# A new order for the same 1738 steps of a decaying linear attention with a feed-forward block behind it

## The chip, the cores and the metric

The kernel runs on one core of a Trainium2 chip. What counts is the time of one execution on the device, in microseconds (us). Three executions of the kernel before took 564.64, 563.89 and 563.01 us; the median is 563.89 us.

A core has a matrix engine (TensorE, PE in the profile), a vector engine (VectorE, DVE), an engine for activation functions (ScalarE, ACT), a general one (GpSimd, POOL) and one that here only issues transfers (SyncE, SP). Each works through its own queue of instructions in order and waits where an instruction needs something that another engine or a transfer has not delivered yet.

## The reference

Attention with a complex, per-position decay is a recurrence over 768 positions, for 4 sequences and 8 heads of 48 dimensions. What comes out is turned into 3072 tokens of 384 features and goes through a feed-forward block with 2048 hidden features.

```
a_n = a * min(|a|, 0.999) / (|a| + 1e-6)          # complex a = a_re + i a_im
for t in range(S):
    S_re, S_im = a_n[t] * (S_re + i S_im) + k[t] v[t]^T
    y[t] = einsum('bhd,bhde->bhe', q[t], S_re)
x = y.transpose(0, 2, 1, 3).reshape(B * S, H * D)
h = x @ w_in
out = (h * (1 / (1 + exp(-1.702 * h)))) @ w_out
```

## The kernel before

**Units.** The 3072 tokens are cut into 12 units of 256 tokens, three to a sequence, each of two chunks of 128 (c = 0 and 1). For every unit the kernel turns the recurrence into matmuls: `prepare` scales and rotates queries and keys by running products and running angles of the decay (scans, L356, L376 and L396 on VectorE; logarithms and sines on ScalarE). Ten transfers (`remap`, L447 to L450), here called the moves, then bring queries and keys of all heads into place in `qkh`. `attend` (L455 on) does the rest for each chunk: 32 small matmuls per half of the heads give the scores (L511, into `p_ps` and `z_ps`), VectorE masks them (`pm`, L517), eight transposes turn the keys (L530), ScalarE copies them (`kt`, L534), small matmuls mix the masked scores and the state with the values into `x_ps` (L501), and others build the new state in `z_ps` (L553, taken over at L569 or L573; the decay of the state is L472). `x_ps` is copied out at L559 and, for the lower half of the precision, at L563. TensorE splits an fp32 matmul into two records in the trace.

**Feed-forward block.** `moe` works on groups of units: unit 0 alone, unit 1 alone, then pairs. Its hidden blocks (L650, into `h_ps0` and `h_ps1`) and its projections (L681, into `o_ps0` to `o_ps2`) are the large matmuls: 128 columns in group 0, 256 in group 1, 512 in the five others. "H1.3" is the hidden block numbered 3 of the group that begins with unit 1. Group 0 uses whole fp32 weights. From group 1 on each weight is split into a high part (L267, ScalarE) and a low part (L272, VectorE), each value of the hidden layer likewise into `gh` (L663) and `gl` (L667), and three products are summed. The silu is at L659 for group 0 and at L663 and L665 for the others.

**Weights.** Sixteen raw blocks of weights, called f0 to f15, are loaded at L245 into four raw buffers in turn and converted there by VectorE (L247, L250, L254) and ScalarE (L253). f11 takes the buffer that f7 had, f13 that of f9.

**What sets the order.** Every piece of work is handed to a plan as a step with its engine, what it reads and what it writes; there are 1738. A table, `ORDER`, lists their numbers. `Plan.order` reads the table and makes sure that no step stands ahead of one that it needs; the loop at the end emits the steps in that order. Each engine's queue is therefore the table, reduced to the steps of that engine; a step of SyncE issues one load or all five transfers of one half of the moves. Where the table of ScalarE's functions has to change between two steps, a load of it (L881) is put in. Thirteen warm-up matmuls (L432) with no use for the result stand ahead of TensorE's work.

```
for n in order:
    o = plan.ops[n]
    if o[5] not in (None, cur):
        nc.scalar.preload_act_table_set(o[5])
        cur = o[5]
    o[3]()
```

## Time and profile before

| | |
|---|---|
| three executions | 564.64, 563.89, 563.01 us; median 563.89 |
| span of the profiled execution | 563.3 us |
| TensorE busy | 527.2 us, 94% |
| VectorE busy | 389.4 us, 69% |
| ScalarE busy | 370.5 us, 66% |
| first matmul starts | 23.10 us |
| last large matmul ends | 558.6 us |
| loads of ScalarE's function tables | 58, 74.4 us in all |

The profile is of one execution. Its page gives busy times and shares for each engine; a matmul's end is modelled, so the duration of a group of matmuls is best read from the starts of what comes before and after. A row of a timeline gives a start, a duration, engine and line, what was written from what, how many, and in brackets how long the engine had stood idle just before and for whom. [...]

### The profile page before, as it was taken

The page shows a single profiled execution, that of the slowest core. Times are in us where ns is not written, and L with a number is a line of the kernel's source. Part 1 is how long each engine was busy: PE and PEld are TensorE (multiplying, and loading weights), DVE is VectorE, ACT ScalarE, POOL GpSimd, SP SyncE. Part 2 cuts the span into 40 slices and gives each one's busy share as a digit, 9 for nine tenths or more (in the row PEclk, how much of TensorE's full clock was granted, in tenths as well). Part 3 has the DMA queues.
Part 4 walks back from the last instruction along what each step waited for, and adds up shares of the span by engine and source line. Part 5 has one row for each costly group of instructions (what it writes and reads, how often), then busy time and mean ns, then how long its engine had stood idle before and what let it go on. Part 6 is the DMA issues. An engine that isn't in the chain of part 4 may idle for free.

```text
span 563.3 us, 14541 instructions
## 1 busy us (share of the span) xinstructions
PE 527.2 (94%) x6204; PEld 447.8 (79%) x6204; DVE 389.4 (69%) x625; ACT 370.5 (66%) x561; POOL 12.0 (2%) x55
## 2 busy tenths in 40 slices
PE   0379799999999999999999999999999999999996
PEld 0368799999988887888888888888888888888885
DVE  7999899999989886977857756654685442243223
ACT  7888789999798979687769667355944221323321
POOL 6000000000000000000000000000000000000000
PEclk9999989999999999999999999999999999999999
DMA  8579993727275756576257355336417013231001
GB/s 333 170 210 358 189 363 68 238 58 197 91 183 189 178 168 171 198 171 201 77 129 243 105 131 162 115 78 154 151 61 185 29 45 101 65 96 45 29 28 61
DMA packets 29270, 82.04 MB, mean 146 GB/s; under 512 B 4112, under 2 KB 7184, under 8 KB 29200
## 3 DMA queue, kind: packets, MB, share of 16 engines
q1 hardware_dynamic: 29200, 81.06, 49.5%
q8 instruction: 50, 0.82, 0.6%
q14 instruction: 20, 0.16, 0.1%
HBM read 57.41 MB, written 4.72 MB: 110 GB/s over the span
## 4 chain that ended last, share of the span: by engine, by line
PE 60%; ACT 1%; DVE 1%; issue 0%; ACTq 0%
PE o_ps L681 26%; PE h_ps L650 25%; PE x_ps L501 4%; PE z_ps L511 1%; PE p_ps L511 1%; PE z_ps L553 1%; PE p_ps L530 1%; PE z_ps L530 1%; DVE qr L229 0%; DVE qk L229 0%; DVE gl L667 0%; ACT L881 0%; ACT h_ps L665 0%; ACT s L333 0%; ACT s L331 0%
## 5 line engine op out<-in xcount | busy, mean ns | idle before, releaser
L667 DVE TENSOR_TENSOR gl<-h_ps,gh 128x512 fp32r<-128x512 f32 x88 | 60.1, 687 | 116.4 <-ACT h_ps L665 113.0
L663 ACT ACTIVATE gh<-h_ps 128x512 fp32r<-128x512 f32 x88 | 52.4, 596 | 133.9 <-PE h_ps L650 105.7
L650 PE MATMUL h_ps<-xhi,hiA 128*128 128x512 f32 (+1 forms) x288 | 109.0, 379 | 0.5 <-DVE gl L667 0.5
L650 PE MATMUL h_ps<-xlo,hiA 128*128 128x512 f32 (+1 forms) x288 | 107.2, 372 | 0.0
L650 PE MATMUL h_ps<-xhi,loA 128*128 128x512 f32 (+1 forms) x288 | 107.1, 372 | 0.0
L681 PE MATMUL o_ps<-gh,hiU 128*128 128x512 f32 (+1 forms) x288 | 80.5, 380 | 0.0
L681 PE MATMUL o_ps<-gl,hiU 128*128 128x512 f32 (+1 forms) x288 | 80.2, 379 | 0.0
L681 PE MATMUL o_ps<-gh,loU 128*128 128x512 f32 (+1 forms) x288 | 78.2, 372 | 0.0
L881 ACT ACT_TABLE_LOAD x58 | 74.4, 1283 | 1.9 <-PEq L1126 0.9
L650 PEld LDWEIGHTS h_ps<-xhi,hiA 128*128 128x128 f32 x288 | 54.2, 188 | 11.1 <-DVE gl L667 1.1
L650 PEld LDWEIGHTS h_ps<-xhi,loA 128*128 128x128 f32 x288 | 54.2, 188 | 9.6
L650 PEld LDWEIGHTS h_ps<-xlo,hiA 128*128 128x128 f32 x288 | 54.3, 188 | 9.2 <-DVE xlo L563 0.3
L681 PEld LDWEIGHTS o_ps<-gh,loU 128*128 128x128 f32 x288 | 52.2, 188 | 9.8
L681 PEld LDWEIGHTS o_ps<-gh,hiU 128*128 128x128 f32 x288 | 51.0, 188 | 11.0 <-issue 2.0
L681 PEld LDWEIGHTS o_ps<-gl,hiU 128*128 128x128 f32 x288 | 50.9, 188 | 9.7 <-issue 0.8
L665 ACT ACTIVATE h_ps<-h_ps 128x512 f32<-128x512 f32 x88 | 51.8, 591 | 0.1
L229 DVE TENSOR_TENSOR qk<-qk,s 128x768 f32<-128x768 f32 (+2 forms) x39 | 43.9, 1133 | 3.2 <-ACT s L425 2.2
L501 PE MATMUL x_ps<-pm,v 128*32 128x128 f32 x768 | 38.9, 276 | 1.4 <-DVE pm L517 1.4
L715 DVE TENSOR_REDUCE fit<-raw_w 128x1 f32<-128x384 f32 x64 | 33.6, 543 | 5.2 <-DMA raw_w<-in_w_out_dram 5.2
L501 PE MATMUL x_ps<-qkh,st 96*32 96x128 f32 x640 | 33.0, 272 | 0.0
L681 PE MATMUL o_ps<-g,valU 128*128 128x128 f32 x192 | 26.3, 289 | 4.3 <-ACT g L659 3.2
L432 PE MATMUL h_ps<-qk,ident 128*128 128x256 f32 x26 | 8.0, 456 | 23.1 <-DVE s L415 23.1
(104 smaller groups left out, 778.6 us busy)
## 6 DMA issues: line engine op xcount, KB each, us to landing
v<-in_v_dram SPq DMA_DIRECT2D x24, 416.0 KB, 4.0
ri<-in_a_dram SPq DMA_DIRECT2D x11, 768.0 KB, 5.9
qk<-in_qk_dram SPq DMA_DIRECT2D x11, 768.0 KB, 6.8
qkh<-qr SPq DMA_DIRECT2D x22, 288.6 KB, 5.9
qkh<-qk SPq DMA_DIRECT2D x22, 288.6 KB, 5.5
raw<-in_w_in_dram SPq DMA_DIRECT2D x8, 768.0 KB, 6.5
raw<-in_w_out_dram SPq DMA_DIRECT2D x8, 768.0 KB, 5.6
raw_w<-in_w_in_dram SPq DMA_DIRECT2D x16, 384.0 KB, 3.5
```

Source lines behind the costliest of these rows:

```text
L229: add(en, t, rank, lambda: e.tensor_tensor(out=out, in0=a, in1=b, op=alu), **kw)
L432: add("PE", 0.43, -WARM + k, lambda k=k, dst=dst: mm(h_ps[0][:, k % 2 * T : (k % 2 + 1) * T], lhsT=ident, rhs=dst[:, k % NR, 0:T], start=T ...
L501: mm(x_ps[32 * j : 32 * j + 32, r, :], lhsT=lt, rhs=rt, start=n == 0, stop=n == len(steps) - 1)
L511: mm(ps_[to : to + QL, j, lo:L], lhsT=at(h, 1, c)[:, lo : lo + QL], rhs=at(h, 0, c)[:, lo:L], start=True, stop=True)
L530: nc.tensor.transpose(banks[h // 4][0][:, h % 4, 0:KD], at(h, 1, c), ident[0:KD, 0:KD])
L650: mm(h_ps[hb][:, k * n_x : (k + 1) * n_x], lhsT=ww[:, r * T + f * P : r * T + (f + 1) * P], rhs=x[:, r, xs], start=n == 0, stop=n == last)
L663: add("ACT", a_t(CW) - 0.13, rk(order_), lambda hb=hb, gb=gb: act(out=high.g(gb), in_=h_ps[hb], func=AF.Silu, scale=SLOPE), r=[f"h{hb}"], ...
L665: add("ACT", a_t(CW) - 0.13, rk(order_), lambda hb=hb: act(out=h_ps[hb], in_=h_ps[hb], func=AF.Silu, scale=SLOPE), w=[f"h{hb}"], tab=SILU, ...
L667: add("DVE", d_t(CW), rk(order_), lambda hb=hb, gb=gb: dve.tensor_tensor(out=glo[gb], in0=h_ps[hb], in1=high.g(gb).bitcast(F32), op=ALU.su ...
L681: mm(o_ps[c][:, xs], lhsT=y[:, f * DM + c * P : f * DM + (c + 1) * P], rhs=x[:, k * n_x : (k + 1) * n_x], start=i == 0 and f == 0 and n == ...
L715: add("DVE", d_t(CK), rk + 2, lambda x=x, op=op: dve.tensor_reduce(out=f_w[:, x, n : n + 1], in_=weights.looked_at()[:, :, 1], op=op, axis ...
L881: nc.scalar.preload_act_table_set(o[5])
```

## The change

The table `ORDER` is replaced by another permutation of the same step numbers that keeps every dependency. Nothing else is touched: the same steps, tiles, buffers and, but for waits and one more table load (59 instead of 58), the same instructions. Two lines of the table, of 73:

```diff
 ORDER = """
-80 5 128 0 100 10 82 81 84 83 85 86 6 87 7 8 94 129 88 9 130 92 89 25
...
+80 5 128 10 100 0 82 81 84 83 85 86 8 6 7 87 88 9 89 90 92 25 94 130
...
```

Three places in which the queues differ follow. In all rows the number behind a name is that of the buffer or tile.

SyncE's queue ahead of the moves of unit 1 (the last five rows of each piece are their first half; `raw_72` to `raw_75` are the four raw buffers; the second `raw_75` from `in_w_in_dram` is f11, `raw_72` and `raw_74` from `in_w_out_dram` are f8 and f10). Before:

```order
L245 DMA raw_75<-in_w_in_dram 128x1536
L324 DMA ri<-in_a_dram 128x1536
L245 DMA raw_72<-in_w_out_dram 128x1536
L607 DMA v_86<-in_v_dram 128x832
L245 DMA raw_74<-in_w_out_dram 128x1536
L245 DMA raw_75<-in_w_in_dram 128x1536
L447 DMA qkh_76<-qr 48x1539 x2
L448 DMA qkh_76<-qr 32x2x513
L450 DMA qkh_76<-qr 16x513 x2
```

and in the new order:

```order
L382 DMA qk<-in_qk_dram 128x3x512
L324 DMA ri<-in_a_dram 128x1536
L245 DMA raw_73<-in_w_in_dram 128x1536
L245 DMA raw_75<-in_w_in_dram 128x1536
L245 DMA raw_72<-in_w_out_dram 128x1536
L245 DMA raw_74<-in_w_out_dram 128x1536
L447 DMA qkh_76<-qr 48x1539 x2
L448 DMA qkh_76<-qr 32x2x513
L450 DMA qkh_76<-qr 16x513 x2
```

f11 has moved from the last place ahead of the moves to a place ahead of f8 and f10, behind f9 (`raw_73`); the load of the values of unit 1 (`v_86`) has gone behind the moves.

VectorE's queue at the hidden block H1.3, which overwrites `h_ps_108` and reads the low half of the weight block A3 (`loA_1319` before, `loA_1122` now). Before:

```order
L472 TENSOR_TENSOR st_93<-st_93,qkh_77 96x4x2x48
L272 TENSOR_TENSOR loU_1280<-valU_482,hiU_568 128x768
L667 TENSOR_TENSOR gl_100<-h_ps_108,gh_1224 128x512
L229 TENSOR_TENSOR qk<-qk,s_83 128x3x256
L415 TENSOR_SCALAR s_82<-s_85 128x3
L272 TENSOR_TENSOR loA_1319<-valA_257,hiA_695 128x768
L229 TENSOR_TENSOR qk<-qk,s_81 128x3x256
```

and in the new order:

```order
L272 TENSOR_TENSOR loA_1122<-valA_233,hiA_534 128x768
L699 TENSOR_SCALAR osb_101<-o_ps_109 128x256
L409 SCALAR_TENSOR_TENSOR s_85<-s_85,s_82 128x3x256
L699 TENSOR_SCALAR osb_103<-o_ps_111 128x256
L699 TENSOR_SCALAR osb_102<-o_ps_110 128x256
L667 TENSOR_TENSOR gl_99<-h_ps_107,gh_1129 128x512
L356 SCALAR_TENSOR_TENSOR s_81<-s_84,s_83 128x257 x3
L364 TENSOR_SCALAR small<-s_81 128x3
L365 RECIPROCAL small<-small 128x3
L376 SCALAR_TENSOR_TENSOR s_83<-s_84,small,s_83 128x256 x3
L517 TENSOR_TENSOR pm_95<-p_ps,mask 128x512
L667 TENSOR_TENSOR gl_100<-h_ps_108,gh_1168 128x512
```

The low half of A3 has moved from the third row behind `gl_100` to the first row here, eleven ahead of it.

TensorE's queue at unit 6, chunk 1 (`qkh_77`): its scores for the second half of the heads (`z_ps`). Before, with 27 large matmuls since the last small one:

```order
L681 MATMUL o_ps_110<-gh_1224,loU_1818 128x512
L681 MATMUL o_ps_110<-gl_100,hiU_1121 128x512
L511 MATMUL z_ps<-qkh_77 32x128 x4
L511 MATMUL z_ps<-qkh_77 32x96 x4
L511 MATMUL z_ps<-qkh_77 32x64 x4
L511 MATMUL z_ps<-qkh_77 32x32 x4
L650 MATMUL h_ps_107<-xhi_926,hiA_756 128x512
L650 MATMUL h_ps_107<-xlo_92,hiA_756 128x512
L650 MATMUL h_ps_107<-xhi_926,loA_1085 128x512
```

and in the new order:

```order
L511 MATMUL p_ps<-qkh_77 32x128 x4
L511 MATMUL p_ps<-qkh_77 32x96 x4
L511 MATMUL p_ps<-qkh_77 32x64 x4
L511 MATMUL p_ps<-qkh_77 32x32 x4
L501 MATMUL x_ps<-pm_96,v_86 32x128 x4
L511 MATMUL z_ps<-qkh_77 32x128 x4
L511 MATMUL z_ps<-qkh_77 32x96 x4
L511 MATMUL z_ps<-qkh_77 32x64 x4
L511 MATMUL z_ps<-qkh_77 32x32 x4
L681 MATMUL o_ps_109<-gh_1129,hiU_1109 128x512
L681 MATMUL o_ps_110<-gh_1129,hiU_1109 128x512
L681 MATMUL o_ps_111<-gh_1129,hiU_1109 128x512
```

The scores of both halves (`p_ps`, `z_ps`) now stand in one row with the end of the mix of the chunk before (`x_ps`), and large matmuls come only behind them.

## Rows read from the trace of the kernel before

**Rows 1.** The page, busy time and share of the span.

```profile
PE 527.2 (94%) x6204; PEld 447.8 (79%) x6204; DVE 389.4 (69%) x625; ACT 370.5 (66%) x561; POOL 12.0 (2%) x55
```

**Rows 2.** Stretches: length, busy time of each engine, granted clock, share of transfers, GB/s.

```profile
70.40:74.00 3.60, 3.30 (x16) 3.30 (x17) 3.60 (x6) 3.57 (x6) 0.17 (x2) 0.53 0.75 215
74.00:117.00 43.00, 42.94 (x784) 41.44 (x785) 40.75 (x59) 39.59 (x60) 0.64 (x3) 1.00 0.61 204
117.00:200.00 83.00, 82.98 (x1279) 72.85 (x1270) 78.56 (x120) 75.70 (x108) 0.54 (x7) 1.00 0.56 151
...
220.00:558.60 338.60, 338.60 (x3338) 278.58 (x3337) 190.78 (x322) 177.64 (x279) 0.83 (x11) 1.00 0.39 110
```

**Rows 3.** The chain that ended last, in order of time: start, us, what.

```profile
402.62 2.04 PE h_ps L650 x9
404.66 0.69 PE p_ps L511 x32
405.36 0.56 PE z_ps L511 x32
405.92 1.32 PE x_ps L501 x48
407.24 2.26 PE h_ps L650 x9
...
423.44 0.33 PE z_ps L530 x4
...
438.70 0.68 PE z_ps L553 x48
```

**Rows 4.** Timeline of TensorE, about 66 to 75 us and at 119 us.

```profile
65.97 0.83 PE L681 MATMUL o_ps<-g,valU 128*128 128x128 f32 x6
66.64 0.83 PE L650 MATMUL h_ps<-x,valA 128*128 128x128 f32 x6
70.70 3.75 PE L681 MATMUL o_ps<-g,valU 128*128 128x128 f32 x18 [3.23 <-ACT g L659]
74.38 0.77 PE L511 MATMUL p_ps<-qkh 96*32 96x128 f32 x32
...
119.11 0.28 PE L650 MATMUL h_ps<-xhi,hiA 128*128 128x256 f32 x1
119.23 0.28 PE L650 MATMUL h_ps<-xlo,hiA 128*128 128x256 f32 x1
```

**Rows 5.** Timeline of VectorE, single rows from 47 to 119 us.

```profile
47.32 0.96 DVE L229 TENSOR_TENSOR qk<-qk,s 128x768 f32<-128x768 f32 x1 [1.01 <-DMA qk<-in_qk_dram]
...
67.82 0.56 DVE L247 TENSOR_SCALAR valA<-raw 128x768 int32<-128x768 int32 x1 [2.51 <-DMA raw<-in_w_in_dram]
...
75.23 0.69 DVE L517 TENSOR_TENSOR pm<-p_ps,mask 128x512 f32<-128x512 f32 x1 [1.01 <-PE p_ps L511]
...
108.46 1.76 DVE L396 TENSOR_TENSOR_SCAN s<-runs,s 128x771 f32<-128x771 uint8 x1 [0.60 <-ACT s L351]
...
112.58 2.02 DVE L376 TENSOR_TENSOR_SCAN s<-s,small,s 128x256 f32<-128x256 f32 x3
...
115.38 0.54 DVE L472 TENSOR_TENSOR st<-st,qkh 96x384 f32<-96x384 f32 x1
...
116.72 0.68 DVE L667 TENSOR_TENSOR gl<-h_ps,gh 128x512 fp32r<-128x512 f32 x1
...
118.25 0.94 DVE L272 TENSOR_TENSOR loA<-valA,hiA 128x768 fp32r<-128x768 f32 x1
```

**Rows 6.** Timeline of SyncE: loads issued at L245.

```profile
56.63 0.33 SPq L245 DMA_DIRECT2D raw<-in_w_in_dram  x1
...
71.20 0.35 SPq L245 DMA_DIRECT2D raw<-in_w_in_dram  x1
```

**Rows 7.** Timeline of ScalarE at the landing of f11.

```profile
67.82 0.92 ACT L253 ACTIVATE raw<-raw 128x768 int32<-128x768 uint32 x1 [2.87 <-DMA raw<-in_w_in_dram]
```

**Rows 8.** The page, transfers: issues, KB each, us from issue to landing.

```profile
raw<-in_w_in_dram SPq DMA_DIRECT2D x8, 768.0 KB, 6.5
```

## The prediction

> **What bounds the kernel now.** I read the page first, then the table of stretches, the chain of waits, and the timelines of single engines where the stretches change character. TensorE (PE) is busy 527.2 of 563.3 us [rows 1], so at first sight every microsecond taken out of TensorE's work comes off the end. The stretches say otherwise for the first third [rows 2]. From 220 us on VectorE (DVE) is busy only 190.78 of 338.60 us and TensorE all of it: there TensorE alone sets the pace. But from 74 to 117 us DVE is busy 40.75 of 43.00 us and ScalarE (ACT) nearly as long, and from 117 to 200 us DVE still 78.56 of 83.00. In these stretches engines are full side by side: whichever has less work up to their next meeting point waits for the other. TensorE's work taken out early is then worth nothing unless VectorE comes early too.

> So two things are to be priced: what one change between large and small matmuls costs, and how early the two engines reach the place from which only TensorE counts.

> **One visit to the small matmuls.** Call a visit an excursion from the large matmuls (L650, L681) to scores, mixes or states and back. The chain shows what it costs beyond its own matmuls [rows 3]: nine hidden matmuls take 2.04 us inside a run and 2.26 us as the first after a visit (+0.22); 32 scores take 0.56 us inside a visit and 0.69 us as its first piece (+0.13). That is 0.35 to 0.36 us per visit. Transposes that stand alone show hardly any of it and are left out. Counted in the listed instructions, visits of this kind go from 48 to 31 while every matmul count stays the same: 17 x 0.36 = 6.1 us less TensorE time. How much of that reaches the end depends on where the visits lie.

> [...]

> **The meeting point.** I take the fourth hidden block of group 1 (H1.3). In the kernel before it starts at 119.11 us [rows 4], right when VectorE has written the low half that it needs (L272, from 118.25 for 0.94, [rows 5]); VectorE's input before that, the difference gl at L667, was done at 116.72 + 0.68 = 117.4 [rows 5]. In the new order that low half stands further ahead, and gl is the last thing that H1.3 needs from VectorE. Ahead of this gl VectorE has the same instructions as before but for three: one L272 more (0.94), one pm (L517, 0.69) and one decay (L472, 0.54) fewer [rows 5], together -0.3 us. So at VectorE's old pace H1.3 can start at 117.1 instead of 119.1: **-2.0 us**.

> What TensorE still has to do from H1.3 on changes little. Visits left go from 36 to 21 (-15 x 0.36 = -5.4). Against that the new order has put off other work to after this point: 18 matmuls of 256 columns (0.12 us each by two starts in [rows 4], +2.1), 8 transposes (0.33 for 4 in [rows 3], +0.7), 24 state matmuls (48 records in 0.68 us, [rows 3], +0.7) and 24 mix matmuls (48 records in 1.32 us, [rows 3], +1.3), together +4.8. Net **-0.6 us**.

> **VectorE's pace.** The rest depends on VectorE's idle time ahead of this point. The largest piece of it comes from a chain of queues. SyncE (SP) issues the weight load f11 at 56.63, just ahead of the moves that bring unit 1's queries and keys into place [rows 6]; it had to wait for its raw buffer, its transfer then shares the queue with those moves, and it lands at 67.8. VectorE waits 2.51 us for it [rows 5], ScalarE 2.87 [rows 7]; ScalarE's silu stands behind that, so TensorE idles 3.23 us [rows 4], and the clock granted afterwards is 0.53 [rows 2], that is mostly the lower of its two levels: 18 records that take 2.0 us at the price of [rows 4] (six in 0.67) take 3.7.

> In the new order f11 is issued ahead of f8, f10 and the moves. Its buffer comes free with the last conversion step of f7, which VectorE reaches after 4.3 us less work (here and below: the instructions listed ahead, at the time from start to start that their like take in the trace) and 1.0 us less waiting, so at about 56.6 - 5.3 = 51.3; the loads of this kind land 6.5 us after their issue in the median [rows 8], and little else is then under way. It lands at about 57.8 or earlier. Its first reader on VectorE has 7.2 us less work ahead of it and comes at 65.3 - 7.2 - 1.0 = 57.1. The 2.51 us go, but for 0.7 at the worst. So does the wait of 1.01 us for qk at 47.32 [rows 5]: its reader now stands behind 5.7 us more of VectorE's work, while the load has one more weight load ahead of it, worth about 2 us. **-3.5 us.**

> What is late next there is unit 1's move itself. It landed just ahead of 74 us and let the scores start at 74.38 [rows 4]; VectorE waited 1.01 us for them until 75.23 [rows 5]. I expect it at the same time or a little earlier: what VectorE writes for it comes after 0.9 us more work and 1.0 us less waiting. VectorE now has 5.3 us more work ahead of these scores' pm (two scans, L396 and L376, of 1.76 and 2.02 us [rows 5], one conversion step, one low half), so it arrives at 75.2 + 5.3 - 3.5 - 1.0 = 76.0 and doesn't wait. A conversion of the next load, f13, now stands directly ahead of that pm; this is the place that the last rival prices.

> **The sum.** -2.0 - 0.6 - 3.5 = -6.1 us against the profiled run, whose span of 563.3 lies 0.6 below the median of 563.89. Carried to the median: **557.8 us**.

> TensorE's own side gives an earlier time, so it is not what ends last: from unit 1's first scores on it has 16 visits fewer (-5.8) and 30 records of 128 columns fewer (0.112 each, -3.4) left, and if these scores start at 74.4 as before, the end comes at 563.9 - 9.1 = 554.8. Between the two the later wins: VectorE, by 3 us. What the new order adds ahead of that (a mix right behind the transposes whose copies it needs, all thirteen warm-up matmuls ahead of the first scores, one table load more) lies beside VectorE's work and is covered while TensorE has those 3 us in hand; uncovered, it would cost one or two us.

> **The rivals.**
> *TensorE's side decides* (VectorE loses still more of its idle time): 554.8, or 553.5 if the moves land 1.3 us earlier. For it: VectorE has other small waits early on; against it: nothing in the order removes them.
> *VectorE idles as long as before.* Each engine works through its queue in order, so a wait removed at f11 can return at the next load or the next scores, as the 1.01 us at 75.23 shows on a small scale. Then only -2.0 - 0.6 remain: 561.3.
> *Visits are free* (the weight load is hidden, and the +0.35 us come from how ends are modelled). Then the work put off costs +4.8 with nothing against it: -2.0 - 3.5 + 4.8 = -0.7, 563.2, no change that shows. For it: ends of matmuls are modelled. Against it: the chain's pieces follow from starts.
> *Slower: VectorE is held at f13.* Its conversion now stands ahead of the pm of unit 1's scores, and its load behind the moves in SyncE's queue. It was issued at 71.20 before [rows 6]. If it is held until the moves have landed (73.8) and then takes as long as f11 did (11.2 us), it lands at 85.0, 9.0 us after VectorE's arrival at 76.0, and the end is at 566.8. It has eaten up the whole gain from a landing at 82.1 on. Against it: f12 stood ahead of it in the kernel before, and VectorE showed no wait for it there; now only the moves stand ahead.

> **How the numbers follow.** The forecast 557.8 gets 0.50, TensorE's side 0.08, VectorE's old idle time 0.20, free visits 0.10, f13 late 0.10, and 0.02 is left for gains and losses that cancel. A measurement can tell about 0.3% from no change, so faster means below 562.2 and slower above 565.6: faster 0.78, same 0.12, slower 0.10. The range leaves out the slow case and part of the free visits: 553.5 at the end where TensorE decides, 563.0 at the other.

> **What would show it.** In the new profile: no DVE or ACT wait for a raw load of w_in between 50 and 70 us, and no stretch with a lowered clock there; H1.3 starting near 113.6 right after gl; TensorE without idle time from there on; 0.35 us still paid at each visit that is left; and VectorE without a wait at about 76 us. A wait of VectorE for f13, a new TensorE idle time of 3 us followed by a lowered clock, or first matmuls after a visit that cost less than 0.1 us more than the others would make the prediction wrong.

## The result, and the profile after

The new order takes 568.52 us in the median (568.10 to 569.59), the order before on the same chip 563.45 (562.56 to 564.64): ratio 1.0094, interval 1.0076 to 1.0113. It is slower by 5.1 us, where 557.8 had been forecast. The profiled execution has a span of 566.1 us; in all kernels here an execution takes about 1.9 us more than its span.

The page, busy time and share of the span, answers to [rows 1]. TensorE is busy for 2.4 us less than before, VectorE for 3.7 and ScalarE for 1.9 us more:

```profile
PE 524.8 (93%) x6204; PEld 450.1 (80%) x6204; DVE 393.1 (69%) x625; ACT 372.4 (66%) x562; POOL 12.1 (2%) x55
```

So TensorE lost time by waiting. Its timeline around the first scores of unit 1 (start, us, what; idle time before it and for whom in brackets) shows four waits of over 0.5 us for VectorE's and ScalarE's part of group 0, three of them ahead of the first scores, which start at 77.32 instead of 74.38 [rows 4]:

```profile
65.93 0.94 PE L681 MATMUL o_ps<-g,valU 128*128 128x128 f32 x6 [1.26 <-DVE valU L254]
69.98 0.94 PE L681 MATMUL o_ps<-g,valU 128*128 128x128 f32 x6 [1.10 <-ACT g L659]
76.45 0.94 PE L681 MATMUL o_ps<-g,valU 128*128 128x128 f32 x6 [1.52 <-DVE valU L254]
77.32 0.76 PE L511 MATMUL p_ps<-qkh 96*32 96x128 f32 x32
...
85.53 1.60 PE L681 MATMUL o_ps<-g,valU 128*128 128x128 f32 x12 [0.53 <-DVE valU L254]
...
115.06 0.39 PE L650 MATMUL h_ps<-xhi,hiA 128*128 128x256 f32 x1
```

The last row is H1.3 (119.11 before, [rows 4]). On VectorE the two rows that matter there: f11 is converted without a wait (before: 2.51 us, [rows 5]), and the difference gl, after which H1.3 starts, ends at 115.00:

```profile
59.05 0.55 DVE L247 TENSOR_SCALAR valA<-raw 128x768 int32<-128x768 int32 x1
...
114.32 0.68 DVE L667 TENSOR_TENSOR gl<-h_ps,gh 128x512 fp32r<-128x512 f32 x1
```

Then comes something that no row of before answers to. Near 182 us TensorE has just done a burst of small matmuls (a new state, a mix and both halves of the scores, 176 records in 3.7 us) and stands in the middle of a projection, in a row of three matmuls that read the same tiles. After the first of the three it stops for 2.96 us:

```profile
180.84 0.74 PE L511 MATMUL z_ps<-qkh 96*32 96x128 f32 x31
181.51 0.96 PE L681 MATMUL o_ps<-gl,hiU 128*128 128x512 f32 x3
182.31 0.39 PE L681 MATMUL o_ps<-gh,hiU 128*128 128x512 f32 x1
185.66 1.22 PE L681 MATMUL o_ps<-gh,hiU 128*128 128x512 f32 x2 [2.96 <-issue]
```

"issue" is time in which the engine waited for nothing that the profile shows. Stretches around it (length, busy time of each engine, granted clock as a share of full speed, share of transfers, GB/s):

```profile
177.00:182.70 5.70, 5.70 (x184) 4.71 (x183) 4.88 (x7) 5.61 (x8) 0.00 (x0) 1.00 0.72 138
182.70:185.66 2.96, 0.00 (x1) 0.00 (x0) 2.96 (x7) 2.90 (x5) 0.00 (x0) 0.98 0.86 224
185.66:189.00 3.34, 3.33 (x8) 2.66 (x9) 2.36 (x5) 1.11 (x2) 0.13 (x2) 0.50 0.74 194
```

TensorE does nothing for 2.96 us and then runs 3.34 us at a granted clock of 0.50 (1.00 ahead of the stall), which by an estimate from these two numbers loses half of that, 1.7 us: 4.6 us together, nearly as much as the whole result.

A table for the rest. At four places both orders have sent exactly the same matmuls to TensorE; the time at which the next one starts there can be compared directly (worked out from the starts of TensorE's records; visits made in each part stand in brackets):

```
                      ahead of H1.0   behind H2.6    behind O6.7   in O10.15
before, profiled      101.32 (10)     188.62 (11)    374.69 (18)   557.71 (9)
after                 102.34 (9)      193.97 (7)     379.20 (10)   560.30 (5)
after, 50 small ones  103.02 (9)      189.84 (7)     374.94 (10)   556.04 (5)
```

The third line is the new order without its stall (below). From H1.0 on it takes 453.02 us, the order before 456.39: a gain of 3.4 with 16 visits fewer.

### The profile page after: what moved, and what is told of

The parts are those of the page before. It is cut to its first block, busy times and chain, and to the rows that moved or that the text cites. A ratio compares the mean times of both kernels' runs of the same rounds, so it can differ in the third digit from the quotient of the medians.

```text
span 566.1 us, 14511 instructions
## 1 busy us (share of the span) xinstructions
PE 524.8 (93%) x6204; PEld 450.1 (80%) x6204; DVE 393.1 (69%) x625; ACT 372.4 (66%) x562; POOL 12.1 (2%) x55
## 4 chain that ended last, share of the span: by engine, by line
PE 66%; ACT 5%; DVE 2%; issue 1%; DMA 1%; ACTq 0%
PE o_ps L681 28%; PE h_ps L650 27%; PE x_ps L501 5%; ACT L881 2%; PE z_ps L553 2%; PE p_ps L511 2%; PE z_ps L511 2%; PE p_ps L530 1%; PE z_ps L530 1%; ACT gh L663 1%; ACT h_ps L665 1%; DMA raw_w<-in_w_in_dram 1%; DVE fit L715 0%; DVE gl L667 0%; ACT s L329 0%
## 5 line engine op out<-in xcount | busy, mean ns | idle before, releaser
L667 DVE TENSOR_TENSOR gl<-h_ps,gh 128x512 fp32r<-128x512 f32 x88 | 60.0, 686 | 100.4 <-ACT h_ps L665 88.5
L663 ACT ACTIVATE gh<-h_ps 128x512 fp32r<-128x512 f32 x88 | 52.4, 597 | 115.7 <-PE h_ps L650 69.6
L650 PE MATMUL h_ps<-xhi,hiA 128*128 128x512 f32 (+1 forms) x288 | 109.0, 379 | 0.8 <-DVE gl L667 0.8
L650 PE MATMUL h_ps<-xlo,hiA 128*128 128x512 f32 (+1 forms) x288 | 107.3, 372 | 0.0
L650 PE MATMUL h_ps<-xhi,loA 128*128 128x512 f32 (+1 forms) x288 | 107.2, 372 | 0.0
L681 PE MATMUL o_ps<-gh,hiU 128*128 128x512 f32 (+1 forms) x288 | 80.2, 379 | 3.3 <-issue 3.0
L681 PE MATMUL o_ps<-gl,hiU 128*128 128x512 f32 (+1 forms) x288 | 79.9, 378 | 0.0
L681 PE MATMUL o_ps<-gh,loU 128*128 128x512 f32 (+1 forms) x288 | 78.8, 374 | 0.0
L650 PEld LDWEIGHTS h_ps<-xhi,hiA 128*128 128x128 f32 x288 | 54.4, 189 | 11.6 <-DVE gl L667 1.8
L681 PEld LDWEIGHTS o_ps<-gh,hiU 128*128 128x128 f32 x288 | 51.5, 189 | 14.0 <-issue 3.8
L650 PEld LDWEIGHTS h_ps<-xhi,loA 128*128 128x128 f32 x288 | 54.4, 189 | 9.7
L650 PEld LDWEIGHTS h_ps<-xlo,hiA 128*128 128x128 f32 x288 | 54.4, 189 | 9.0
L681 PEld LDWEIGHTS o_ps<-gh,loU 128*128 128x128 f32 x288 | 52.7, 190 | 9.7
L681 PEld LDWEIGHTS o_ps<-gl,hiU 128*128 128x128 f32 x288 | 51.2, 188 | 9.3 <-issue 0.4
L501 PE MATMUL x_ps<-pm,v 128*32 128x128 f32 x768 | 40.2, 275 | 1.0 <-DVE pm L517 0.6
L715 DVE TENSOR_REDUCE fit<-raw_w 128x1 f32<-128x384 f32 x64 | 33.0, 543 | 11.4 <-DMA raw_w<-in_w_in_dram 6.3
L681 PE MATMUL o_ps<-g,valU 128*128 128x128 f32 x192 | 25.5, 280 | 5.3 <-DVE valU L254 4.2
L432 PE MATMUL h_ps<-qk,ident 128*128 128x256 f32 x26 | 8.2, 492 | 23.7 <-DVE qk L229 23.7
```

The costliest lines, as they stand in the source:

```text
L501: mm(x_ps[32 * j : 32 * j + 32, r, :], lhsT=lt, rhs=rt, start=n == 0, stop=n == len(steps) - 1)
L650: mm(h_ps[hb][:, k * n_x : (k + 1) * n_x], lhsT=ww[:, r * T + f * P : r * T + (f + 1) * P], rhs=x[:, r, xs], start=n == 0, stop=n == last)
L663: add("ACT", a_t(CW) - 0.13, rk(order_), lambda hb=hb, gb=gb: act(out=high.g(gb), in_=h_ps[hb], func=AF.Silu, scale=SLOPE), r=[f"h{hb}"], ...
L667: add("DVE", d_t(CW), rk(order_), lambda hb=hb, gb=gb: dve.tensor_tensor(out=glo[gb], in0=h_ps[hb], in1=high.g(gb).bitcast(F32), op=ALU.su ...
L681: mm(o_ps[c][:, xs], lhsT=y[:, f * DM + c * P : f * DM + (c + 1) * P], rhs=x[:, k * n_x : (k + 1) * n_x], start=i == 0 and f == 0 and n == ...
L715: add("DVE", d_t(CK), rk + 2, lambda x=x, op=op: dve.tensor_reduce(out=f_w[:, x, n : n + 1], in_=weights.looked_at()[:, :, 1], op=op, axis ...
```

## The stall near 186 us

**Theory.** TensorE's instructions arrive by transfer too, and the packet of them that it stood still for came late. The page lists a queue of instructions:

```profile
q8 instruction: 50, 0.82, 0.6%
```

50 packets of 16 KB, beside 12408 matmuls and weight loads: 248 of these to a packet. Three idle times of TensorE in this profile are put down to "issue", 2.96 us at 185.66, 0.45 at 283.56 and 0.20 at 304.48. By TensorE's recorded instructions (its semaphore instructions among them) they stand right behind number 4801, 7105 and 7617, 9 and 2 times 256 apart. By an estimate from these distances a packet holds 256, and 248 leaves out the semaphore instructions and those without a record.

Counted against TensorE's starts, a packet begins as a rule when some 220 instructions are still in hand (median), 0.6 us after TensorE has begun on the last packet that it has. The packet at 182.9 us begins 4.3 us after that and with none in hand: the 176 small matmuls with their weight loads use up 352 instructions in 3.7 us, while unit 5's moves keep the transfer engines busy (0.72 and 0.86 above). By the same count the order before never has fewer than 87 in hand when a packet begins.

**Moves later.** SyncE's two steps for unit 5's moves (770, 772) go behind a later load (1623):

```diff
-... 770 758 ... 772 914 ... 1623 734 ...
+... 758 ... 914 ... 1623 770 772 734 ...
```

> The changed order, with one thing else in SyncE's queue: the ten moves of unit 5, issued from 177.0 us on in the changed kernel, stand behind the next look at the weights, which is issued only when VectorE has done its previous look (183.1 us). TensorE's queue is the same. Theory 'instructions come late': TensorE's own instructions arrive as pieces of 16 KB by transfer, and the piece wanted during the run of small matmuls ahead of 182.7 us stood behind these moves; with the moves later it arrives in time, the idle time of 2.96 us in the middle of a projection (L681) at 185.66 goes, and the lowered clock after it (3.4 us at half, 1.7 us): 568.5 - 4.7 = 563.8. Rival 'a wait of the matmul's own' (an operand that the profile does not name): no change, 568.5 within 0.5, and the idle time is still in the middle of that projection.

Measured 567.81 (ratio 1.0068, 1.0043 to 1.0092). The packet now begins 0.7 us after TensorE has begun on the last one, the projection runs through and no clock is lowered there:

```profile
184.73 0.85 PE L681 MATMUL o_ps<-gh,hiU 128*128 128x512 f32 x3
```

TensorE is 4.8 us better between its 2300th and 2390th record. But 3.4 us of that are lost again up to its 3000th, and this execution had lost 2.4 us at the first hidden block already. Two of the new waits are one for the load of the values, which stands behind the moves in SyncE's queue and so went out later too, and one without a releaser:

```profile
201.34 0.84 PE L553 MATMUL z_ps<-v,kt 128*32 128x48 f32 x45 [1.08 <-DMA v<-in_v_dram]
208.19 0.50 PE L681 MATMUL o_ps<-gl,hiU 128*128 128x512 f32 x1 [1.04 <-issue]
```

**Scores apart.** The scores of unit 4, chunk 1, leave the burst and stand one projection later:

```diff
-... 724 732 912 772 914 596 733 915 601 ...
+... 912 772 914 596 915 601 724 732 733 ...
```

> The changed order, with the scores of unit 4's second chunk (both halves, 64 records) and their mask taken out of the run of small matmuls ahead of 182.7 us and put behind the next six matmuls of a projection and the three ahead of them. The moves stay where they are. Theory 'instructions come late': TensorE now takes its instructions more slowly while the piece is on its way (128 fewer in the same time), so the idle time of 2.96 us shrinks to below 1 us or goes, and the lowered clock with it; one visit more costs 0.25 to 0.36: 568.5 - 4.7 + 0.3 = 564.1, at the least 2 us less than 568.5. Rival 'a wait of the matmul's own': the projection starts earlier and waits as long as before, 568.5 + 0.3.

Measured 568.25 (1.0088, 1.0059 to 1.0117). The stall shrank to 1.61 us, with no lowered clock behind it, and it now stands within the scores that were put off:

```profile
187.70 0.26 PE L511 MATMUL z_ps<-qkh 96*32 96x32 f32 x5 [1.61 <-issue]
```

2.1 us had been lost early again. Both runs pointed to the instruction supply but hardly changed the time, so the next ones change nothing but the count.

**Useless matmuls ahead.** Ahead of the first warm-up, while TensorE has nothing to do (until 23.7 us), N matmuls of one element:

```diff
-add("PE", 0.43, -WARM + k, lambda k=k, dst=dst: mm(
+add("PE", 0.43, -WARM + k, lambda k=k, dst=dst: ([mm(h_ps[0][0:1, 0:1], lhsT=ident[:, 0:1], rhs=ident[:, 0:1],
+    start=True, stop=True) for _ in range(N * (k == 0))], mm(
```

All else stands in its old order; only the place where the instruction stream is cut moves, four instructions for each: two records (the profile with N = 50 has 100 of them) and their two weight loads.

N = 50: 

> The new order unchanged; ahead of the first warm-up, while TensorE has nothing to do (it starts at 23.7 us), 50 useless 1x1 matmuls are added (100 records of TensorE, 200 instructions with their weight loads). Every later step, wait and transfer keeps its place; only the boundaries of the 256-instruction pieces in which TensorE's instructions are fetched move by 200. Instruction supply theory: the stall of 2.96 us in the middle of projection O2.4 (185.7 us) and the lowered clock behind it come from a piece whose fetch began just as a burst of small matmuls started, beside unit 5's moves; with this shift no fetch falls at the start of a burst beside moves, no such idle time is left, and the time is 568.5 - 4.7 = 563.8 (about 1 us more or less for the early part, which differs from run to run). Rival, the idle time belongs to that matmul (its weights, its bank, its wait): the stall stays, 568.5.

Measured 563.89, before 562.84 beside it (1.0018, 1.0001 to 1.0035). With 50 useless matmuls more the kernel is 4 us faster: +1.0 against before instead of +5.1. The place of the stall, in its profile:

```profile
182.20 0.96 PE L681 MATMUL o_ps<-gl,hiU 128*128 128x512 f32 x3
183.00 0.85 PE L681 MATMUL o_ps<-gh,hiU 128*128 128x512 f32 x3
183.69 0.84 PE L681 MATMUL o_ps<-gh,loU 128*128 128x512 f32 x3
```

Its packets begin at 180.8 and 185.5 us here, with 201 and more instructions in hand.

N = 2, a control: 

> A control for the kernel with 50 useless matmuls ahead of the warm-ups: the same with 2 of them, 8 instructions. Instruction supply theory: the piece of instructions is cut only 8 places earlier, its fetch still begins as the burst of small matmuls starts beside unit 5's moves; the stall of about 3 us near 186 us stays, 568.5. Rival, the useless matmuls help by being there (an engine or a clock that is awake early, a queue that is primed): 564, no stall.

Measured 572.36 (1.0161, 1.0138 to 1.0185). The stall is there, and longer, with 6.8 us at a granted clock of 0.50 around it (the profile has another 3.4 us of that at 78.5, and the mean granted clock of all four executions is as low, 0.988 to 0.989):

```profile
181.61 0.74 PE L511 MATMUL z_ps<-qkh 96*32 96x128 f32 x31
186.17 1.65 PE L681 MATMUL o_ps<-gl,hiU 128*128 128x512 f32 x3 [3.82 <-issue]
```

It now comes ahead of the first matmul of the projection and not behind the fourth. Four matmuls and four weight loads are 8 instructions, which is just what the two useless ones (two records each, with a weight load to each) have put ahead. The stall belongs to a place in the instruction stream, not to a matmul.

The profiles of all kernels bear this out. They show 19 idle times of TensorE of over 0.25 us that are put down to "issue", in ten kernels. Count TensorE's recorded instructions (matmuls, weight loads and its own semaphore instructions, the useless ones too): every one of these idle times stands right behind number 4801, as the stall does, or a whole multiple of 256 away from it (3009 to 9921), whether a projection, a score or a mix comes next. Each ends 2.3 to 3.0 us after a packet has begun.

Not only the moves hold packets up. Call a packet due when TensorE begins on the last one that it has. In the 18 profiles, behind 60 us, 272 packets fell due while no transfer of the kernel was under way, and none began more than 1.5 us later; 544 fell due beside a transfer, and 117 of them began more than 2.5 us later.

N = 24: 

> As the kernel with 50, but with 24 useless 1x1 matmuls (96 instructions). Instruction supply theory: by the starts of TensorE's records in the profile of the new order, the fetch at 178 us then falls even worse (short by 85 instructions instead of level), and two others fall at the start of a burst beside moves, near 122 us (short by 67) and near 217 us (short by 57): three idle times put down to no one (issue) in the trace near 125, 185 and 220, 2 to 4 us each, with or without a lowered clock behind them; 570 to 577. Rival, the idle time belongs to the matmul: one stall of 2.96 us at the old place, 568.5.

Measured 565.55 (1.0046, 1.0027 to 1.0064): a miss, faster than the new order and not slower. The stall at 186 us is gone, where it should have grown; of the two others only the first appeared, small:

```profile
126.50 0.27 PE L501 MATMUL x_ps<-qkh,st 96*32 96x128 f32 x1 [0.62 <-issue]
```

The packet began at 177.7 us, just ahead of the moves (issued from 178.3 us on), and so wasn't held up. That a shift would move the stalls could be foreseen, but not where a packet would be held up.

## The price of a visit

Twelve visits of the order before, between 330 and 480 us, are split in two: one block of large matmuls (below 1057 and 1069, hidden blocks) is taken forward into each visit, so that the visit's last group comes behind it.

```diff
-... 1247 1057 1246 ... 1263 1065 1256 1066 1408 1257 1069 ...
+... 1057 1247 1246 ... 1263 1065 1069 1256 1066 1408 1257 ...
```

> The kernel before, with twelve visits to the small matmuls cut in two between 330 and 480 us, where TensorE had no idle time: one hidden block or projection is taken forward into the visit, every matmul stays. Prediction's price (0.36 us a visit): + 4.3 us. The price that the two profiles give when the time from each start to the next is summed by what follows (0.09 going in, 0.15 to 0.18 coming out, about 0.25): + 3.0 us. Rival 'visits are free': 0.

Measured 567.99 (1.0079, 1.0054 to 1.0104), and between TensorE's 4000th and last record 4.25 us more: 0.354 us for each visit. The price of the prediction, 0.36, holds for visits that are added; they are not free.

This profile showed something else. Up to 330 us its queues are those of the order before, but its stall at 70 us is not there:

```profile
68.34 0.83 PE L650 MATMUL h_ps<-x,valA 128*128 128x128 f32 x6
69.43 2.27 PE L681 MATMUL o_ps<-g,valU 128*128 128x128 f32 x18 [0.25 <-ACT g L659]
71.64 0.77 PE L511 MATMUL p_ps<-qkh 96*32 96x128 f32 x32
...
116.36 0.28 PE L650 MATMUL h_ps<-xhi,hiA 128*128 128x256 f32 x1
```

The first scores come at 71.64 instead of 74.38, H1.3 at 116.36 instead of 119.11 [rows 4], and VectorE doesn't wait for f11. Of nine profiles with this early order (seven from the sections below) two have that wait, the profiled one of before and one more. H1.0 starts at 98.7 us in their median, in nine profiles with the new early order at 103.3.

## The early part

**Old early part, new rest**, joined at H1.3, and the other way round:

> The order before up to hidden block H1.3, the remaining steps in the new order: 33 visits instead of 48. If the late part of the new order is good but for its stall, and the early part is what loses: 563.4 - 15 x 0.354 = 558.1 without the stall, 562.8 with the stall and its lowered clock (4.7), which should stay since every late record keeps its number. If the late part of the new order loses by itself (more than its visits give): 566 or later.

> The new order up to hidden block H1.3, the remaining steps in the order before: 47 visits. If the early part brings little and puts 4.8 us of work off: H1.3 starts between 115.1 and 117.5, and what is left takes 445 + 4.8, so the span is 565 to 567.5 and the time 567 to 569, as slow as the new order without its saved visits. If the early part gains what was predicted (5.5 us for 4.8 put off) and the new order's loss lies behind H1.3: 562.8.

Measured 566.96 (1.0077, 1.0048 to 1.0106) and 570.18 (1.0113, 1.0081 to 1.0144). The first reaches H1.0 at 97.8, but TensorE then waits for VectorE at 119.3 and 122.9 us (0.62 and 1.84, with a lowered clock behind: 0.97 in the mean from 117 to 180 us), and at its 1600th record it stands at 134.95, the new order at 135.12. Its stall is there at the same matmul of the same projection (3.10 us). Both kernels lose at the seam, which makes them inconclusive on the whole time. In the first, the early start is used up by waits for VectorE; whether the new order without a seam could keep it isn't shown.

**Conversion of f10 ahead**, in the kernel with 50 useless matmuls (VectorE's queue; ScalarE's step of f10 goes ahead in its own):

```diff
-... 51 270 459 461 462 466 59 52 54 ...
+... 51 52 54 459 461 462 466 270 59 ...
```

> The new order with 50 useless matmuls (no stall), in which VectorE ends the conversion of f10 (steps 52 and 54) ahead of two scans of unit 2 and the low half of A0 instead of behind them, and ScalarE does its part of f10 ahead of the high half of A0: TensorE's wait of 1.54 us for that conversion, the last ahead of unit 1's first scores (77.9 us), goes. Theory, VectorE works without idle time up to hidden block H1.3 and sets its start: the first scores start 1.5 us earlier or more, H1.3 still starts at 115.7 and the time stays 563.9. Rival, what TensorE gains ahead of unit 1's scores reaches the end: H1.3 at 114.2, 562.4.

Measured 563.74 (1.0002, 0.9988 to 1.0015). The wait ahead of unit 1's first scores is gone, and the scores start at 77.05 instead of 77.99, although this execution was 0.8 us late by then. H1.3 starts at 116.66 instead of 115.73, so nothing of that has arrived there:

```profile
77.05 0.77 PE L511 MATMUL p_ps<-qkh 96*32 96x128 f32 x32
...
80.77 0.55 PE L530 MATMUL p_ps<-ident,qkh 96*128 96x96 f32 x4 [0.55 <-DVE pm L517]
...
84.09 0.94 PE L650 MATMUL h_ps<-x,valA 128*128 128x128 f32 x6 [0.81 <-DVE valA L254]
...
116.66 0.38 PE L650 MATMUL h_ps<-xhi,hiA 128*128 128x256 f32 x1
```

The 1.5 us come back as 0.55 and 0.81 at once. VectorE sets the pace up to H1.3, as the expectation said. Stretches of 75 us up to there, first the new order, then the order before as in the profile without the f11 wait:

```profile
40.00:115.00 75.00, 69.40 (x1061) 65.77 (x1059) 73.62 (x102) 66.80 (x94) 1.38 (x7) 1.00 0.72 234
```

```profile
40.00:115.00 75.00, 72.25 (x1166) 68.52 (x1165) 72.47 (x102) 67.63 (x98) 1.27 (x5) 1.00 0.75 238
```

VectorE is full in both, with as many instructions (102). But TensorE gets 2.9 us more done beside it in the old order. The new one has put matmuls off behind H1.3, and what TensorE saves by that is idle time.

**Decide early.** The last small matmul (L753) waits 1.59 us at the end; its steps go ahead of the last projections:

```diff
-... 1597 1598 ... 1732 1600 1733 ... 1734 1613 1735 ...
+... 1597 1732 1733 1734 1735 1598 ...
```

> The changed order, with VectorE's last look (L732, L735), the judgement (L748, L749) and GpSimd's step taken forward by four gl steps, to where the kernel before has them; TensorE's last tiny matmul (L753) then waits for nothing. Theory 'the verdict is read at the end': the changed kernel has the verdict 1.2 us later after its last large matmul than the kernel before (563.11 - 561.15 against 559.34 - 558.56), and every engine reads it before it ends: 568.5 - 1.2 = 567.3, and the time beyond the span shrinks. Rival: the last output transfer ends the kernel anyway (span only 0.25 us longer in its tail): 568.5, no change.

Measured 569.39 (1.0093, 1.0066 to 1.0121): no gain. The wait is gone, but the last output transfer ends the kernel: it lands at 565.6 of 567.5 us, and at 564.0 of 566.1 in the new order. The stall was there again, 2.97 us at the same matmul.

## Whether saved visits reach the end

Three kernels begin in the old order and turn to the new one at a later place, where both have sent (nearly) the same matmuls. In two more the other engines' queues turn some 15 us earlier than TensorE's.

> The order before up to the end of hidden block H2.6 (188.6 us; at this point both orders have sent the same matmuls), the remaining steps in the new order: 36 visits, 12 fewer than before, and neither the early part of the new order nor its stall. If the late part of the new order keeps what its saved visits give: 563.0 - 12 x 0.354 = 558.8, or up to 1.9 later, by what the new order gave back to waits between this place and projection O6.7: 558.8 to 560.7. Rival, the late part is worth nothing by itself: 563.0.

> The order before up to hidden block H2.13 (229.8 us; the same matmuls have been sent by then but for two blocks), the remaining steps in the new order: 38 visits, 10 fewer than before. VectorE stands one step behind the new order at the seam and ScalarE one ahead, so that little is late there. If saved visits reach the end where no other engine is late: 0.354 each, 563.5 - 3.5 = 560.0, plus 0.7 to 1.7 for the waits of the new order near 270 and 300 us (0.7 in its own profile, 1.7 behind the seam at H2.6): 560.7 to 561.7. Rival, every seam gives back what the visits save: 563.5.

> The order before up to hidden block H6.8 (375.1 us; both orders have sent the same matmuls), the remaining steps in the new order: 44 visits, 4 fewer than before, all in a stretch in which TensorE has no idle time in either order. If visits have their price there: 563.5 - 4 x 0.354 = 562.1; by the two profiles this stretch takes 183.0 us in the order before and 181.1 in the new one, which gives 561.6. Rival, ScalarE or VectorE, seven steps behind the new order at the seam, hold TensorE up: 563.5 or later.

> As the kernel that turns to the new order at H6.8 (375.1 us): TensorE's queue is the same, 44 visits. But the queues of the other engines turn to the new order 18 us earlier, at projection O6.3 (356.8 us), where VectorE is idle four tenths of the time, so that the seven steps by which VectorE was behind are done by the time TensorE turns. If the 8.67 us of that kernel were the seam's and saved visits reach the end: 563.5 - 1.9 = 561.6, with TensorE idle nowhere behind 375 us and 181.1 us from there to the last projection instead of 183.0. Rival, merging the last visits makes VectorE late by itself: an idle time before a hidden block near 384 us again, 565 or later.

> As the kernel that turns to the new order at H2.13 (229.8 us): TensorE's queue is the same, 38 visits. The queues of the other engines turn at projection O2.9 (214.9 us), 15 us earlier. If the 2.12 us idle and the lowered clock at 234 us in that kernel were the seam's: 563.5 - 10 x 0.354 = 560.0, plus 0.7 to 1.3 for the small waits near 270 and 285 us that every kernel with this late part shows: 560.7 to 561.3. Rival, the seam's price is only moved: 563.5 or later.

```
turn at            visits  time     ratio (interval)            idle time at the seam
H2.6               36      563.97   0.9998 (0.9979 to 1.0017)   1.36 and 0.71
H2.13              38      567.63   1.0060 (1.0035 to 1.0084)   2.12
H2.13, others 15   38      566.92   1.0058 (1.0038 to 1.0078)   2.05 and 1.22
H6.8               44      573.77   1.0180 (1.0153 to 1.0207)   8.67
H6.8, others 18    44      578.18   1.0255 (1.0220 to 1.0290)   9.02 and 2.71
```

All miss. In the H6.8 kernel TensorE waits for gl, and VectorE ahead of it for two loads that the new order, run from its start, has behind it by then (L715, the reading of raw weights for their range):

```profile
383.61 0.80 PE L650 MATMUL h_ps<-xhi,hiA 128*128 128x512 f32 x1 [8.67 <-DVE gl L667]
```

```profile
377.37 1.01 DVE L715 TENSOR_REDUCE fit<-raw_w 128x1 f32<-128x384 f32 x2 [3.15 <-DMA raw_w<-in_w_out_dram]
381.94 1.01 DVE L715 TENSOR_REDUCE fit<-raw_w 128x1 f32<-128x384 f32 x2 [3.56 <-DMA raw_w<-in_w_out_dram]
```

A turn of the other queues 18 us earlier only moved that wait (9.02 us at 366.5). One thing the profiles agree on: from O6.7 to O10.15 TensorE takes 181.10 us in the new order and in all of these whose seam lies ahead of it, and 183.02 before, with four visits fewer and no idle time in either. There saved visits do reach the end, 1.9 us for four.

So the last kernel has no seam: the order before, and in TensorE's queue alone five visits behind 350 us are put off until they stand ahead of the next one (TensorE's queue at two of them):

```diff
-... 1263 1256 1257 1069 1067 1068 1260 ... 1434 1427 1121 1122 1129 1429 ...
+... 1069 1067 1068 1263 1256 1257 1260 ... 1121 1122 1129 1434 1427 1429 ...
```

> The order before, in which only TensorE's queue is changed, and only behind 350 us: five visits are put off by 4 to 12 us until they stand directly ahead of the next one (units 8 to 11), so that 43 visits are left instead of 48. The queues of the other four engines are word for word those of the order before. If saved visits reach the end where nothing else is late: 563.5 - 5 x 0.354 = 561.7. Rival, the states, mixes and scores that come later hold VectorE, ScalarE and then TensorE up: 563.5 or later, with an idle time of TensorE behind 350 us.

Measured 566.13 (1.0056, 1.0032 to 1.0080), slower again. Where nothing waits the price holds: TensorE is 0.38 us better behind the first merged visit (near 351 us). But the second one had stood between hidden blocks and the projection that needs their silu. There the old order has

```profile
377.50 0.43 PE L501 MATMUL x_ps<-pm,v 128*32 128x128 f32 x8
...
379.64 0.97 PE L681 MATMUL o_ps<-gh,hiU 128*128 128x512 f32 x3
```

and the merged one, with the clock lowered from 377.5 to 380.9 us behind it:

```profile
377.04 1.28 PE L681 MATMUL o_ps<-gl,hiU 128*128 128x512 f32 x3 [1.84 <-DVE gl L667]
```

The visit of 2.1 us had given ScalarE and VectorE the time for silu and gl. Without it TensorE waits, once 1.84 us with 1.7 more for the clock, once 1.45 (401.8). That is more than five visits are worth. No version beat the order before.

## Why the prediction was wrong

Against an undisturbed execution of before (H1.0 at 98.6) the four places give: 3.8 us late at H1.0 (4.6 by the medians), 4.6 for the stall, 3.4 gained back: 5.0 to 5.8, measured 5.1. That the stall cost its 4 us is shown by the kernel with 50 useless matmuls; why the new early part is late is argued from the timelines alone.

Against the sum itself, which gives a span of 557.2, the profiled execution with 566.1 is 8.9 us late: 1.5 at H1.3, 7.2 behind it, of which the stall is 4.6, and 0.2 at the very end.

**A visit costs 0.36 us**: right for visits added, 0.354. But the sum let all of it count for visits saved. From H1.0 on 16 visits fewer gave 3.4 and not 5.8: TensorE's own time fell by 4.3, which is 0.27 a visit, and waits of 0.2 to 0.5 us, most of which the order before doesn't have, took 0.9 of it. Why a saved visit gave 0.27 there and 0.48 behind O6.7 stays open. A visit is also cover for the engines beside it, as the merged kernel shows; this side of it the sum didn't have.

**f11 and VectorE's pace, -3.5**: the mechanism was right, the term was not. f11 is issued at 52.8 and converted without a wait at 59.05, and no lowered clock follows (granted 1.00 from 40 to 115 us). But the wait that it removes was a feature of the profiled execution: seven of nine profiles with that early order don't have it. The sum was made against a span of 563.3 "0.6 below the median", but with the 1.9 us that lie around every span here it belongs to a time of 565.2, above each of the three executions shown. The profiled execution was a late one, and the sum took one of its accidents for a property of the order.

**H1.3 right behind gl, near 113.6**: it starts right behind gl, at 115.06, 1.5 late. Against 119.11 that is -4.1 of the forecast -5.5; against an undisturbed 116.36 only -1.3.

**What is left behind H1.3, -0.6**: in the new order without its stall 440.3 us, before 438.6: +1.7. The 4.8 us put off were real, and the 15 visits paid for less of them than was counted.

**Unit 1's first scores as before or a little earlier**: the move did come earlier, its last transfer landing at 70.6 instead of 73.8, but the scores start 2.9 us later. TensorE's queue ahead of them waits three times for group 0; the last wait, 1.52 us, is for the conversion of f10, which had gone behind two scans and the low half of A0. The prediction added up VectorE's work ahead of one reader and didn't look who else waited in that row. This last wait by itself cost nothing, as the conversion kernel shows; VectorE's total decides.

**TensorE without idle time from H1.3 on**: the step that failed most. It took for granted that TensorE does its listed matmuls back to back when operands are there, and gave nothing for it. In its place stand the 2.96 us of the stall and the 1.7 us of the lowered clock. It is the very sign that the prediction had named as one against itself, but no rival had a cause for it. A merged burst beside transfers is what the instruction supply couldn't follow (352 instructions in 3.7 us, with the packet 4.3 us behind TensorE's start on the last one), and nothing in the profile of before hinted at it except the queue's row. It is no cost of merging as such: the same order, cut elsewhere, has no stall.

Of the rivals none had the cause. "VectorE idles as long as before" named the right doubt, 561.3; "slower" came out, but not by its mechanism, since f13 was not late.

## What to carry to other kernels

When work is taken off an engine, ask what it had covered: a visit to small matmuls between a hidden block and its projection is waiting time put to use, and saving it is worth its price (0.36 us here, against a wait of 1.84 us) only where nothing else comes due. Before costing a stall of the profile, look whether a second execution has it, and whether the profiled one is typical in time. An idle time put down to "issue" in the middle of a row of equal matmuls, behind a burst of small ones and beside heavy transfers, can be a late piece of the instruction stream, as the 2.96 us were here. Two things tell it from a wait of the matmul's own: such idle times stand whole packets (256 here) apart when TensorE's instructions are counted, and useless instructions put ahead of everything move them.
